# Half of the first batch's x turned by DMA inside the weight fold, with two gate-weight conversions begun later

## The chip, the core and the metric

The kernel runs on one core of a Trainium2 chip. The metric is device time in microseconds: the median of 4 runs of the kernel before is 760.85 us (760.52 to 764.25). The profiler records one execution, which took 760.52 us; its span, from the first to the last recorded instruction, is 758.7 us. Engines are TensorE (PE; its weight loads are shown apart as PEld), VectorE (DVE), ScalarE (ACT), GpSimd (POOL) and SyncE (SP), which here only issues DMAs.

## What is computed

The four weight matrices are 64-bit floats, which the kernel reads as pairs of 32-bit words and converts itself; q, k, v, g_norm and the output are 32-bit. Cut to what matters:

```python
# q, k, v: (8 batches, 8 heads, 576 rows, 64); w1, w2: (512, 1024); w3: (1024, 1024); w_out: (1024, 512)
kv  = einsum('bhsd,bhse->bhde', k, v)
o   = einsum('bhsd,bhde->bhse', q, kv)
o   = o / sqrt(mean(o * o, axis=-1) + 1e-6) * g_norm
x   = o.transpose(0, 2, 1, 3).reshape(4608, 512)
out = ((x @ w1) * (x @ w2)) @ w3 @ w_out
```

## The kernel before, in words

**Stages.** The kernel has a fold, then nine groups of 512 rows of x (eight batches of 512 rows, and one group of the rows left over from all batches). The fold computes w3 @ w_out once, so that each group needs only the two gate products and one projection. The fold has two halves of eight chunks each (`c` from 0 to 7 in `fold_chunk(half, c, ...)`, L615). For each chunk TensorE turns four 128x128 blocks of w3 (`turn_w3`, L602), ScalarE copies them out of PSUM (L607), and TensorE makes four products over 512 columns. In the second half the sums of each quarter are copied to `w3o_sb` (L620) when chunk 7 is done.

**Conversion.** Weights come in 64-bit form through four raw buffers and are converted unit by unit (`conversion`). A unit is begun with two ScalarE passes (L158, L159) by `begin_next` and ended with four VectorE passes (L161, L165, L168, L171) and, for gate weights, a scaling by g_norm (L136 on VectorE, L134 on ScalarE for units begun in the first group) by `end_next`. Counted from 0 there are 20 units: eight chunks of w3 and w_out (0 to 7), then w3's second half and the gate weights in turn; 10, 12, 14, 15, 16, 17, 18 and 19 are gate weights (w1 and w2 for one of eight blocks of columns). In the second half of the fold, units 10 to 15 are begun at the head of chunks 0 to 5.

**The first batch.** The second half of the fold also does the attention of batch 0, since the first group needs its x. At chunks 1 and 4, k times v (L334) and the turning of q (L353) are done for two pairs of heads each; at the ends of chunks 2 and 5 the product with kv (L410), `product(0)` and `product(1)`. Its norm runs on ScalarE and VectorE (L378, L379, L383, L385) and ends with VectorE writing xn (L388), in the next chunk. xn must be turned, so that features lie along partitions. Before the change TensorE does this at the ends of chunks 3 and 6 (`turn`, L444: four 128x128 transposes for each of two r), and ScalarE copies the result to xT (L446). xn has one buffer for both halves.

**Turning by DMA.** Later batches turn x in another way (`x_by_dma`, `turn_by_dma`): a copy that sets the two 16-bit halves of each word apart (L291), a DMA transpose issued by SP (L295), and a copy that puts the halves together again (L305). Two such turns, one for each r, run in step. POOL makes the copies. The first transpose overwrites cells that both first copies read, so it waits for both, and the copies behind wait for both transposes.

**Gates and projection.** A group's two gate products are made together by a scheme with seven block products instead of eight (`winograd`, L636). `combine_x(0)` (L678) and `sum_w(p)` (L688, L689) prepare the sums which it needs. The first products are put in one PSUM bank each and copied out (`keep`, L649, tiles p and u) before another product is added on top in the same bank. Of x, the first product needs only the half h = 0, the second t1 (a difference within h = 0), the third t2, which needs both halves.

**Order.** PE, POOL and SP follow the order of the program text everywhere. Inside the fold VectorE and ScalarE do so too. In the first group (T = 0) VectorE and ScalarE are ordered by a scheduler, which weighs when it expects each instruction's inputs; conversions 16 to 19 are done there. SP is one queue: a DMA that must wait holds all behind it.

Of the kernel before, what the change touches and what calls it, by code (L numbers as in the profile page):

```python
# [22 lines left out]
def kernel(  # L23
# [32 lines left out]
    nc = tc.nc  # L56
    PSUM = bass.MemoryType.PSUM
    P = 128
# [5 lines left out]
    KF = DF // P  # L64
    NH = KF // 2
# [17 lines left out]
    def bank(pool, tag):  # L83
        return pool.tile([P, 512], FP32, name=tag, tag=tag)
# [19 lines left out]
    def load_kv_left(b):  # L104
        for t, src in zip(kv_left, (k, v)):
            nc.sync.dma_start(out=t[0:L], in_=src[b, :, G:S, :].rearrange("h p d -> p h d"))

    def load_q_left(b):
        if b % 2 == 0:
            q_left[b // 2] = inp.tile([P, H, D], FP32, name="ql_sb", bufs=1)  # L110
        nc.sync.dma_start(
            out=q_left[b // 2][(b % 2) * L:(b % 2 + 1) * L],
            in_=q[b, :, G:S, :].rearrange("h p d -> p h d"),
        )
# [105 lines left out]
    def conversions(n):  # L220

        what, i = todo[n]
        if what == "w":
            dst = w_sb[:, i].rearrange("p w c f -> p (w c f)")

            return [conversion(n, dst, raws[n], scale=g_col, by_scalar=in_first_group)]
        if what == "b":
            return [conversion(n, chunks[:, 2 * i:2 * i + 2, 0, :], raws[n])]
        dst = chunks[:, i].rearrange("p w f -> p (w f)")
        cuts = [[0, 256, 512, 1024], [0, 512, 1024], [0, 1024]][min(i, 2)]  # L230
        return [conversion(n, dst, raws[n], slice(a, b)) for a, b in zip(cuts, cuts[1:])]
# [4 lines left out]
    def begin_next():  # L236
        if len(begun) < len(todo):
            begun.append(conversions(len(begun)))
            for c in begun[-1]:
                next(c)  # L240

    def end_next(load=True):
        for c in begun[len(converted)]:
            all_of(c)
        converted.append(len(converted))
        if load:
            load_next()

    def all_of(steps):
        for _ in steps:  # L250
            pass
# [16 lines left out]
    def keep_warm(n):  # L268

        t = bank(ps_mm, "mm")  # L270
        for _ in range(n):
            nc.tensor.matmul(t[:, 0:P], lhsT=ident, rhs=ident, start=True, stop=True)

    def turn_by_dma(srcs, apart, turned, dsts, copy=nc.gpsimd.tensor_copy):

        def words(t):
            return t.bitcast(U16).rearrange("p ... (n w) -> p ... n w", w=2)  # L280

        def planes(t, i, n):
            t = t.bitcast(U16).rearrange("p (w n) -> p w n", w=2)
            size = 4 * P // n
            return t[:, :, i * size:(i + 1) * size]

        for i, src in enumerate(srcs):
            to = planes(apart, i, len(srcs))
            if len(src.shape) == 3:
                src, to = words(src), to.rearrange("p w (a n) -> p w a n", a=src.shape[1])  # L290
                copy(to, src.rearrange("p a n w -> p w a n"))  # L291
            else:
                copy(to, words(src).rearrange("p n w -> p w n"))
        yield
        nc.sync.dma_start_transpose(  # L295
            out=turned.bitcast(U16).rearrange("p (a t) -> p a t", t=P), in_=apart.bitcast(U16)
        )
        yield
        for i, dst in enumerate(dsts):
            src = planes(turned, i, len(dsts))  # L300
            if len(dst.shape) == 3:
                src = src.rearrange("p w (a n) -> p a n w", a=dst.shape[1])
            else:
                src = src.rearrange("p w n -> p n w")
            copy(words(dst), src)  # L305

    def together(turns):

        turns = list(turns)
        while turns:  # L310
            turns = [t for t in turns if next(t, turns) is None]
            yield


    def attention(b):
# [129 lines left out]
            dst = xT[b][:, r // 2, :, r % 2, :]  # L445
            copies["xT"] = nc.scalar.copy(dst, t_ps.rearrange("p (i j) t -> p i (j t)", i=2))  # L446

        def x_by_dma(h):

            xn, x = st[h].rearrange("p i l m d -> p (i l) (m d)"), xT[b][:, h]  # L450
            flat = x.rearrange("p i r n -> p (i r n)")
            turned = st[h].rearrange("p i l m d -> p (i l m d)")
            half = [slice(r * G, (r + 1) * G) for r in range(2)]
            return together(
                turn_by_dma(
                    [xn[:, :, r * P:(r + 1) * P]], flat[:, half[r]], turned[:, half[r]], [x[:, :, r]]
                )
                for r in range(2)
            )
# [138 lines left out]
    def turn_w3(half, c):  # L598
        t_ps = bank(ps_at, "at").rearrange("p (m f) -> p m f", m=NH)
        for m in range(NH):  # L600
            src = chunks[:, c, 0, m * P:(m + 1) * P]
            nc.tensor.transpose(t_ps[:, m, :], src, ident)  # L602

        w3T[half, c] = ab[c % 4 // 2][:, c % 2].rearrange(
            "p i (a f) -> p (i a) f", f=P
        )
        nc.scalar.copy(w3T[half, c], t_ps)  # L607
# [3 lines left out]
    def fold_chunk(half, c, ms):  # L611
        if c == 0 and 0 in ms:
            sums_ps[half] = [bank(ps_mm, "mm") for m in range(NH)]
        for m in ms:
            nc.tensor.matmul(  # L615
                sums_ps[half][m], lhsT=w3T[half, c][:, m, :], rhs=chunks[:, c, 1, :],
                start=(c == 0), stop=(c == KF - 1),
            )
            if c == KF - 1:
                nc.scalar.copy(w3o_sb[:, half * NH + m, :], sums_ps[half][m])  # L620
# [573 lines left out]
    with tc.manual_schedule(  # L1194
        engines={mybir.EngineType.DVE, mybir.EngineType.Activation, mybir.EngineType.SP}
    ):
        for _ in range(RAW):
            load_next()
        nc.scalar.activation(const.tile([P, 1], FP32, name="warm"), eps_col, AF.Sqrt)
        g_row = const.tile([1, P], FP32, name="g_row")  # L1200
        for e in range(2):
            nc.scalar.dma_start(
                out=g_row[:, e * D:(e + 1) * D], in_=g_norm.rearrange("(o d) -> o d", o=1)
            )


        keep_warm(14)
        begin_next()
        end_next()
        turn_w3(0, 0)  # L1210
        keep_warm(5)
        begin_next()

        g_ps = bank(ps_at, "at")[:, 0:1]
        nc.tensor.transpose(g_ps, g_row, ident[0:1, 0:1])
        nc.scalar.copy(g_col, g_ps)
        for c in range(KF):

            if c == 0:
                end_next()  # L1220
                begin_next()
            else:
                begin_next()
                end_next()
            if c == 4:
                load_kv_left(0)
                load_pair("kvq", 0, 0)
            elif c == 5:
                load_pair("kvq", 0, 1)
                load_q_left(0)  # L1230
            fold_chunk(0, c, range(NH - 1))
            turn_w3(*((0, c + 1) if c + 1 < KF else (1, 0)))
            fold_chunk(0, c, [NH - 1])
            if c == 0:
                keep_warm(4)


        first = batch(0)
        first.start()
        BEGIN, PRODUCT = {1: (0, 1), 4: (2, 3)}, {2: 0, 5: 1}  # L1240
        norms = {}
        FIRST = len(converted) + KF - 1
        for c in range(KF):
            if c in BEGIN:
                first.begin_kv(*BEGIN[c])
                first.begin_q(*BEGIN[c])
                if c == max(BEGIN):
                    load_q_left(1)
            if c - 1 in norms:
                all_of(norms[c - 1])  # L1250
            if c < KF - 2:
                begin_next()

                end_next(len(raws) < FIRST)
            elif c == KF - 2:
                run(sum_w(0))
            else:
                run(combine_x(0))
                end_next(False)
                for _ in range(3):  # L1260
                    load_next()
            fold_chunk(1, c, range(NH - 1))
            if c + 1 < KF:
                turn_w3(1, c + 1)
            fold_chunk(1, c, [NH - 1])
            if c in PRODUCT:
                norms[c] = first.product(PRODUCT[c])
                next(norms[c])
                next(norms[c])
            if c - 1 in norms:  # L1270
                for r in range(2):
                    first.turn(2 * PRODUCT[c - 1] + r)
    fold_cm.__exit__(None, None, None)
    late_pool = ctx.enter_context(tc.tile_pool(name="late", bufs=1, reuse_waits="tile"))
    allocate()
# [119 lines left out]
```

## Time and profile before

| what | us |
|---|---|
| median of 4 runs | 760.85 |
| profiled execution, time | 760.52 |
| profiled execution, span | 758.7 |
| TensorE matmuls busy | 751.2 |
| VectorE busy | 586.1 |
| ScalarE busy | 262.1 |
| GpSimd busy | 165.7 |
| first gate matmul (L636) starts at | 83.39 |
| the first group's second, third and fourth gate start at | 95.48, 111.69, 124.74 |

Busy time is the sum of the durations of an engine's instructions. The chain of work that ended last is followed back from the last instruction: at each step to what released it, or to the instruction before it on its engine. A line of the timeline has the start, the time, the engine and line, the operation, the tile written and those read, shapes, a count where equal instructions are merged, and in brackets the idle time ahead of it with what ended it. Each matmul of 32-bit data is seen as two passes in the counts. A window's line has for each engine its busy time and number of instructions, then the granted clock, the DMA engines' mean share and GB/s.

### The profile page before, as it was taken

How to read it: one execution, taken by the hardware profiler on the slowest of the kernel's cores; microseconds unless marked ns; L12 is line 12 of the kernel's file. 1: busy time of each engine (PE TensorE's matmuls, PEld its weight loads, DVE VectorE, ACT ScalarE, POOL GpSimd, SP SyncE). 2: the span in 40 equal slices, each digit the busy share in tenths (PEclk: the TensorE clock that was granted, in tenths of full speed). 3: DMA queues.
4: the chain of work that ended last, by engine and by line, in shares of the span. 5: the costliest groups of instructions: out<-in, count | busy, mean ns of one | idle time of the engine just before them, and what ended most of it. 6: DMA issues, size and time to landing. Idle time of an engine off the chain costs nothing.

```text
span 758.7 us, 14978 instructions
## 1 busy us (share of the span) xinstructions
PE 751.2 (99%) x5923; PEld 658.5 (87%) x5923; DVE 586.1 (77%) x1171; ACT 262.1 (35%) x488; POOL 165.7 (22%) x190
## 2 busy tenths in 40 slices
PE   8999999999999999999999999999999999999998
PEld 5455788888899889988998899889988999999997
DVE  7978999539888568847985898467866778996897
ACT  6677776312322332232223322322233223222321
POOL 0000000222510441043104410431053125006100
PEclk9999999999999999999999999999999999999999
DMA  9996843339997836776677566735742470466244
GB/s 322 337 355 190 224 147 77 84 105 260 309 319 256 230 101 165 230 220 133 204 225 226 142 186 228 220 93 161 231 129 56 150 220 39 146 202 194 84 146 146
DMA packets 142330, 142.15 MB, mean 187 GB/s; under 512 B 82356, under 2 KB 129588, under 8 KB 142260
## 3 DMA queue, kind: packets, MB, share of 16 engines
q1 hardware_dynamic: 139808, 126.77, 56.6%
q10 hardware_dynamic: 2452, 14.42, 5.8%
q8 instruction: 47, 0.77, 0.4%
q14 instruction: 23, 0.19, 0.1%
HBM read 105.78 MB, written 19.14 MB: 165 GB/s over the span
## 4 chain that ended last, share of the span: by engine, by line
PE 96%; DMA 2%; ACT 0%; issue 0%; SPq 0%; DVE 0%; ACTq 0%
PE mm L636 55%; PE mm L1065 22%; PE mm L615 7%; PE mm L865 5%; PE at L334 3%; PE at L410 2%; DMA raw<-in_moe_w_out_dram 1%; DMA w3o_sb<-w3o_l 1%; PE at L865 1%; PE at L602 1%; PE at L1116 0%; DMA raw<-in_moe_w_dram 0%; PE at L444 0%; PE at L353 0%; PE at L429 0%; ACT ab L158 0%
## 5 line engine op out<-in xcount | busy, mean ns | idle before, releaser
L636 PE MATMUL mm<-xT,w_sb 128*128 128x256 f32 x720 | 165.2, 379 | 0.0
L636 PEld LDWEIGHTS mm<-xT,w_sb 128*128 128x128 f32 x720 | 136.3, 190 | 18.7 <-issue 0.5
L636 PE MATMUL mm<-xc,ws 128*128 128x256 f32 x512 | 115.7, 379 | 0.0
L636 PEld LDWEIGHTS mm<-xc,ws 128*128 128x128 f32 x512 | 97.2, 190 | 13.3
L291 POOL COPY xT<-xn 128x1024 uint16<-128x1024 uint16 x26 | 31.4, 1236 | 173.8 <-DVE xn L388 173.8
L774 DVE TENSOR_TENSOR c<-mm,u 128x512 f32<-128x512 f32 x32 | 22.0, 688 | 59.8 <-PE mm L636 59.8
L649 ACT COPY u<-mm 128x512 f32<-128x512 f32 x58 | 34.0, 586 | 95.9 <-PE mm L636 85.4
L649 ACT COPY p<-mm 128x512 f32<-128x512 f32 x66 | 38.8, 588 | 74.4 <-PE mm L636 74.4
L615 PE MATMUL mm<-chunks,ab 128*128 128x512 f32 x128 | 60.3, 603 | 1.3 <-ACT chunks L159 0.8
L636 PE MATMUL mm<-xc,w_sb 128*128 128x256 f32 x256 | 61.5, 383 | 0.0
L636 PE MATMUL mm<-xT,ws 128*128 128x256 f32 x240 | 57.4, 382 | 0.0
L775 DVE TENSOR_TENSOR ab<-c 128x256 f32<-128x256 f32 x96 | 54.0, 562 | 2.5
L636 PEld LDWEIGHTS mm<-xc,w_sb 128*128 128x128 f32 x256 | 47.7, 190 | 7.1 <-ACT u L649 0.3
L636 PEld LDWEIGHTS mm<-xT,ws 128*128 128x128 f32 x240 | 45.0, 190 | 6.3
L379 DVE TENSOR_REDUCE inv<-sq 128x8 f32<-128x512 f32 (+1 forms) x40 | 23.4, 627 | 34.6 <-ACT sq L378 34.6
L1065 PE MATMUL mm<-w3o_sb,ab 128*128 128x128 f32 x368 | 48.7, 275 | 0.2 <-DMA w3o_sb<-w3o_l 0.2
L1065 PE MATMUL mm<-w3o_sb,raw 128*128 128x128 f32 x372 | 48.1, 275 | 0.4 <-DMA w3o_sb<-w3o_l 0.4
L1065 PEld LDWEIGHTS mm<-w3o_sb,ab 128*128 128x128 f32 x368 | 45.4, 192 | 0.8 <-issue 0.4
L1065 PEld LDWEIGHTS mm<-w3o_sb,raw 128*128 128x128 f32 x372 | 44.7, 192 | 0.6 <-issue 0.6
L770 ACT COPY c<-mm 128x256 f32<-128x256 f32 x32 | 12.0, 374 | 93.5 <-PE mm L636 93.5
L305 POOL COPY xT<-xn 128x1024 uint16<-128x1024 uint16 x26 | 32.2, 1267 | 54.3 <-DMA xn<-xT 54.3
L1076 ACT COPY u<-mm 128x512 f32<-128x512 f32 x23 | 13.5, 586 | 86.3 <-DVE raw L1089 38.5
(298 smaller groups left out, 1372.6 us busy)
## 6 DMA issues: line engine op xcount, KB each, us to landing
w3o_sb<-w3o_l SPq DMA_DIRECT2D x18, 896.0 KB, 4.7
raw<-in_moe_w_dram SPq DMA_DIRECT2D x31, 512.0 KB, 7.4
raw<-w3o_l SPq DMA_DIRECT2D x15, 896.0 KB, 4.7
w3o_sb<-w3o_l ACTq DMA_DIRECT2D x14, 896.0 KB, 4.8
k_sb<-in_k_dram SPq DMA_DIRECT2D x32, 256.0 KB, 4.2
v_sb<-in_v_dram SPq DMA_DIRECT2D x32, 256.0 KB, 4.6
q_sb<-in_q_dram SPq DMA_DIRECT2D x32, 256.0 KB, 3.8
out_dram<-raw SPq DMA_DIRECT2D x14, 512.0 KB, 5.0
```

The costliest lines, as they stand in the source:

```text
L291: copy(to, src.rearrange("p a n w -> p w a n"))
L305: copy(words(dst), src)
L334: nc.tensor.matmul(kv_ps[e * D:(e + 1) * D, r - rs[0], :], lhsT=k_sb[:, e, cols] if j < J else kl[:, 2 * r + e, :], rhs=v_sb[:, e, cols] i ...
L379: nc.vector.tensor_reduce(out=inv[:, i], in_=sq.rearrange("p (h d) -> p h d", d=D), axis=AX.X, op=ALU.add)
L410: nc.tensor.matmul(o_ps[l][tokens, n * D:(n + 1) * D], lhsT=qT[r][rows, e, i, tokens], rhs=kv_b[rows, e, r, :], start=True, stop=True,)
L615: nc.tensor.matmul(sums_ps[half][m], lhsT=w3T[half, c][:, m, :], rhs=chunks[:, c, 1, :], start=(c == 0), stop=(c == KF - 1),)
L636: nc.tensor.matmul(ps[:, u, :], lhsT=lhsT(a_name, u, c), rhs=rhs(b_name, c),  start=(u == 0 and c == 0 and to is None), stop=(c == chunks ...
L649: copies.setdefault(name, []).append(nc.scalar.copy(t, ps))
L774: nc.vector.tensor_add(c, one, two)
L775: nc.vector.tensor_mul(dst, c[:, 0, :], c[:, 1, :])
L865: nc.tensor.matmul(ps[place // 4][:, place % 4, :], lhsT=x, rhs=y, start=new and place // 4 not in seen, stop=True, skip_group_check=True,)
L1065: nc.tensor.matmul(to[:, i, :], lhsT=x[:, c, :], rhs=y[:, c, :], start=new and place // 4 not in seen, stop=(c == 1), skip_group_check=True,)
```

## The change

Batch 0's first half of x (h = 0) is turned by DMA with ScalarE in place of POOL for the copies: begun at the end of chunk 3 and ended at chunk 5. The turns of the second half move from the end of chunk 6 into chunk 7, behind its first product; `combine_x(0)`, the end of unit 15 and three loads move behind them. Unit 14 is begun in chunk 4 behind `turn_w3`, not at the head of that chunk; unit 15 is begun in chunk 6, not in chunk 5.

```diff
-        def x_by_dma(h):
+        def x_by_dma(h, copy=nc.gpsimd.tensor_copy):
...
                 turn_by_dma(
-                    [xn[:, :, r * P:(r + 1) * P]], flat[:, half[r]], turned[:, half[r]], [x[:, :, r]]
+                    [xn[:, :, r * P:(r + 1) * P]], flat[:, half[r]], turned[:, half[r]], [x[:, :, r]],
+                    copy,
                 )
...
             if c - 1 in norms:
                 all_of(norms[c - 1])
             if c < KF - 2:
-                begin_next()
+                if c < max(BEGIN):
+                    begin_next()
+                if c == max(BEGIN) + 1:
+                    all_of(x_first)
 
                 end_next(len(raws) < FIRST)
             elif c == KF - 2:
                 run(sum_w(0))
-            else:
+            fold_chunk(1, c, [0])
+            if c + 1 == KF:
+                for r in range(2):
+                    first.turn(2 + r)
                 run(combine_x(0))
                 end_next(False)
                 for _ in range(3):
                     load_next()
-            fold_chunk(1, c, range(NH - 1))
+            fold_chunk(1, c, range(1, NH - 1))
             if c + 1 < KF:
                 turn_w3(1, c + 1)
+            if c in (max(BEGIN), KF - 2):
+                begin_next()
             fold_chunk(1, c, [NH - 1])
             if c in PRODUCT:
                 norms[c] = first.product(PRODUCT[c])
                 next(norms[c])
                 next(norms[c])
-            if c - 1 in norms:
-                for r in range(2):
-                    first.turn(2 * PRODUCT[c - 1] + r)
+            if c - 1 == min(PRODUCT):
+                x_first = first.x_by_dma(0, nc.scalar.copy)
+                next(x_first)
+                next(x_first)
```

`max(BEGIN)` is 4, `min(PRODUCT)` is 2, `KF` is 8 and `NH` is 4.

## The prediction

> **What bounds the kernel now.** I read the page first, parts 1 and 4, for the engine that carries the end:
>
> ```profile
> PE 751.2 (99%) x5923; PEld 658.5 (87%) x5923; DVE 586.1 (77%) x1171; ACT 262.1 (35%) x488; POOL 165.7 (22%) x190
> PE 96%; DMA 2%; ACT 0%; issue 0%; SPq 0%; DVE 0%; ACTq 0%
> ```
>
> TensorE is on 96% of the chain that ended last. So an instruction taken off TensorE is worth its own time, and a copy on another engine costs only what TensorE waits for it. Then the chain in order of time around the change (start, length, what, all in us):
>
> ```profile
> 61.80 0.86 PE mm L615 x2
> 62.66 0.95 PE at L444 x8
> 63.61 1.31 PE at L334 x40
> 64.92 1.02 PE at L353 x8
> 65.94 2.58 PE mm L615 x6
> 68.52 0.44 PE at L602 x4
> 68.96 3.68 PE mm L615 x8
> ...
> 79.10 1.01 PE at L444 x8
> 80.11 3.44 PE mm L615 x8
> 83.55 17.28 PE mm L636 x80
> ```
>
> It is unbroken TensorE from 61.8 to 100.8 us; both groups of L444 (the two pairs of turns of x) lie on it. Eight fold matmul passes take 3.44 us undisturbed and 3.68 where a late ScalarE copy (L607) holds the next chunk. Next, ScalarE's and VectorE's lines in order of time, since the change loads the first and delays the second:
>
> ```profile
> 80.67 1.06 ACT L293 COPY qT<-q_sb 128x1024 uint16<-128x1024 uint16 x1
> 91.98 1.15 ACT L134 ACTIVATE w_sb<-w_sb,g_col 128x1024 f32<-128x1024 f32 x1 [0.15 <-DVE w_sb L171]
> 97.41 0.59 ACT L649 COPY p<-mm 128x512 f32<-128x512 f32 x1 [1.35 <-PE mm L636]
> 104.87 2.23 ACT L305 COPY qT<-q_sb 128x1024 uint16<-128x1024 uint16 x2
> 90.72 1.22 DVE L171 CUSTOM_DVE_ANT_0 w_sb<-w_sb,ab 128x2048 uint16<-128x2048 uint16 x1
> ```
>
> They price the new copies (about 1.05 us apart, 2.23 for two), and show a chain used below: the last pass of a gate unit on VectorE (L171) releases ScalarE's scaling (L134), which stands in ScalarE's queue ahead of the copy p out of PSUM. Last, POOL's timeline in batch 1, where the same turn by DMA stands, and the DMA's share in the window 62 to 64 us:
>
> ```profile
> 148.29 2.23 POOL L305 COPY xT<-xn 128x1024 uint16<-128x1024 uint16 x2 [4.27 <-DMA xn<-xT]
> 62.00:64.00 2.00, 2.00 (x25) 1.35 (x25) 2.00 (x3) 2.00 (x4) 0.00 (x0) 1.00 0.00 0
> ```
>
> A pair of DMA transposes takes 4.27 us from the last copy ahead of it to the first behind it, in a stretch with little traffic (share 0.17 from 140 to 160 us). At 62 to 64 us the DMA engines are idle.
>
> **The Trainium skill.** "ScalarE: Activation LUTs", section "What ACT_TABLE_LOAD costs", gives an ACTIVATE with immediate operands 186 ns + 0.833 ns per element: 1,039 ns for 1,024, as an estimate for a copy. The trace agrees for L293 (1.03 to 1.08 us); L305 on ScalarE is slower (1.16 to 1.19). "TensorE: Matmul & The Clock Gate", section "Part 4: PE-mode transpose", says that a turn on TensorE ends in PSUM and needs a copy out; here that is L446, 0.59 us each. "DMA: Bandwidth & Descriptors", section "Issuing engines are not separate DMA queues", says that all DMAs share 16 engines; so new transposes can be late behind loads, and the trace has transposes landing 2.7 to 10.5 us after issue. "Perfetto Trace Analysis", section "Identifying the Most-Contended Engine", warns that matmul busy time overstates TensorE; the chain and the missing gaps are what I rest on.
>
> **The change part by part** (times of before; the instruction order of the changed program is known, its durations are taken from the rows).
>
> 1. Turns 0 and 1 leave TensorE: 8 transposes, the piece of 0.95 us, which includes a wait for xn (L388). Gain 0.95. The copies L446 (two, 1.07 us) go too.
>
> 2. ScalarE gets two L291-type copies after chunk 4's L607: 63.35 to about 65.35. Never seen on ScalarE; L293's 1.05 is the nearest (POOL does L291 in 1.04 to 1.24), bounds 0.95 to 1.25. Behind them in the queue are the kv copies (65.35 to 66.45) and two qT copies (to 67.4). TensorE needs the kv bank for chunk 5's turn at 68.52 − 0.95 = 67.5, so 1.1 us cover it; without that cover each us late is a us lost.
>
> 3. On SP two transposes go in ahead of batch 1's k and v loads. Both copies must be done (they read what the first transpose overwrites): issue at 65.4 and 66.7, both landed at 65.4 + 4.27 = 69.7. SP is then late for k by about 67.9 − 64.26 = 3.6 us. But before, SP waited between these loads (one v issue took 1.81 us, kl and vl came after a pause), so I put the gate-weight loads behind them at about 72 instead of 71.31; k and v are read at 100.8, the first of those weights at 84.5.
>
> 4. Unit 14's begin (L158, L159) moves behind chunk 5's L607. That copy now runs at 67.9 instead of 69.16, before TensorE needs it: the 3.68 shrinks to about 3.5. Gain 0.16. VectorE is not delayed: it is busy with unit 13 until 70.7 in either kernel, and unit 14's L158 is done by 69.5.
>
> 5. ScalarE then has L305 twice from 70.5 to 72.75, ahead of chunk 6's L607 (to 73.35) and of the squares. TensorE needs that L607 at 73.75. So cover is 0.4 us at the copy, and 0.8 us before the DMA (69.7) would be what ScalarE waits for.
>
> 6. Turns 2 and 3 move into chunk 7 behind its first matmul. VectorE runs unit 14 without a break to 75.25, so xn comes only 0.5 us earlier, at about 78.55; TensorE arrives at 78.65. So they run at about the undisturbed 0.87 (1.01 before): gain 0.14. combine_x(0) follows with t1 at 81.1 and t2 at 81.9, needed at 83.9 and 85.6: nothing. First gate matmul: 83.4 − 0.95 − 0.16 − 0.14 = 82.15, 1.25 us earlier.
>
> 7. The first group. Unit 15's begin is now inside the fold (77.4 to 79.5), and the scheduler puts the rest in another order. Each gate's copy p must leave PSUM before its bank takes the third product. In gate 0 the second copy stands behind unit 16's two passes (84.7 + 1.06 + 1.06, then 0.6: done 87.5), needed at 82.15 + 3 × 1.73 = 87.35: loss 0.2. In gate 1 the first p now stands behind unit 16's L134 and unit 18's L158. On VectorE, unit 16's L171 no longer runs at 90.72: unit 15's four passes start at 83.7, and then L161, L136, L165, four ws sums, two c sums and two products come ahead of it; summing their start-to-start times (1.14 for L161 and L171, 0.6 for most, 0.34 for products) it ends at 95.7. Then L134 1.05, L158 1.06, p 0.6: done 98.45. TensorE would want it at about 97.85. Loss 0.6. From there VectorE, without idle time from 84 to 107 us in the profile, is about 0.7 ahead of its old times, and in gate 2 the copy p (114.42 + 0.57 = 115.0, needed at 113.42 + 1.73 = 115.15) has only 0.15 us of slack before, so more than about 0.8 could not come through anyway.
>
> Sum: −0.95 − 0.16 − 0.14 + 0.2 + 0.6 = −0.45. The profiled execution has a span of 758.7 and a time of 760.52, so 1.8 lies around it and is untouched: 760.1 for it. The median, 760.85, is 0.33 above that execution; I predict 760.4 against the median. After the first group the order on all engines is the old one, so I let the shift pass unchanged to the end; a wait of about 1 us for a load in the second group (TensorE waits for w3o_sb near 228 and 231 us) hangs on loads issued from the same chain and should shift along.
>
> **The rivals.**
> A. The whole 1.25 comes through: the waits of step 7 are small sums of many rows and vanish if VectorE is 0.7 us faster than I sum. For it: before, no such wait shows between 83 and 135 us. Against: L171's new place. 760.85 − 1.25 = 759.6.
> B. VectorE or the later loads hold the old times and all is absorbed, or step 7 is worse by 1 us: 760.85 to 761.6. For it: VectorE has no idle time there, and gate 2's 0.15 us slack. Against: it starts this stretch 0.5 earlier.
> C. Slower: ScalarE's queue is blocked at L305 by the DMA transposes, and L607 with w3T of chunk 6 waits behind it. TensorE loses every us beyond 0.8 + 0.4; the change turns slower once the pair lands over 1.2 + 0.45 = 1.65 us late, that is 5.9 us instead of 4.27 after the copies. With the slowest landing in the trace (10.5 us after an issue at 66.7, so 77.2, against 70.9 that costs nothing) it is +6.3 − 0.45: about 766.7. For it: 0.8 us of slack is thin. Against: the idle DMA window, and the k and v loads are issued after the transposes.
> That the change does not act (the copies remain, or the turns) is excluded: the changed program has 8 transposes less on TensorE.
>
> **How the numbers follow.** Forecast 0.45, A 0.24, B 0.17, C 0.10, and 0.04 for a gain that I cannot name. 0.5% is 3.8 us, about what a measurement of this kernel can tell from no change; forecast, A and B all lie within it, and so does C where the pair lands under some 5 us late, for which I leave it 0.02. Faster by more would need waits of over 3.8 us to vanish: the chain has none such after 15 us. So faster 0.04, within 0.88, slower 0.08. The range takes A with a scatter of 0.6 below it (759.0) and B with the same above (762.2); it leaves out most of C. The runs of before scatter from 760.52 to 764.25, so a median may stand somewhat high.
>
> **What would show it.** Right: no L444 near 62 us, 8 transposes at about 78.7; two L291 copies on ScalarE from 63.4; the two DMA transposes issued at about 65.4 and landed by 70; no TensorE gap near 73.7; L636 beginning near 82.2; a TensorE wait of some tenths before gate 1's third product near 98, with L134 in ScalarE's queue ahead of p. Wrong: L305 starting after 71 with DMA as the releaser (C), a first gate at 83 or later (step 5 or 6), or gate 2 starting 1.2 us earlier than 111.7 (A). If the time moves by over 3.8 us the cause lies outside this stretch, and the reading of the chain as TensorE's own time is wrong.

## The result, and the profile after

The changed kernel takes 760.32 us (median; 759.56 to 761.82) against 761.22 for the kernel before (760.03 to 768.68). The ratio is 0.9984, with a 95% interval of 0.9976 to 0.9992: 1.2 us faster, 0.6 to 1.8, within the 0.5% that I set as the bound of a change that can be told. It is close to the ratio of the means (760.38 and 761.58), in which the longest executions weigh; by medians the kernel is 0.90 us faster. The forecast was 760.4. The two kernels' fastest executions lie 0.5 us apart; what differs most is the upper end, and that is where this study ends up.

The page of the changed kernel, parts 1 and 4:

```profile
PE 751.2 (99%) x5915; PEld 658.3 (87%) x5915; DVE 588.4 (78%) x1171; ACT 264.5 (35%) x490; POOL 164.9 (22%) x190
PE 94%; ACT 2%; DMA 2%; DVE 1%; issue 0%; SPq 0%; ACTq 0%
```

Eight matmul instructions fewer, as said, and yet no less TensorE time. ScalarE and VectorE have come onto the chain. The chain in order of time (start, length, what) shows where:

```profile
62.76 0.86 PE mm L616 x2
63.62 1.32 PE at L334 x40
64.94 1.02 PE at L353 x8
65.96 2.58 PE mm L616 x6
...
68.98 3.52 PE mm L616 x8
...
95.75 1.15 DVE w_sb L171
96.92 0.61 ACT w_sb L134
...
97.98 1.15 ACT ab L158
99.12 0.48 ACT p L650
...
99.65 1.99 PE mm L637 x8
```

L444 is gone from between the fold matmul and L334, and 3.68 has become 3.52. The second part is step 7's chain for gate 1, link by link: VectorE's L171, then ScalarE's L134, L158 and the copy p (L650), then TensorE. ScalarE's timeline of the changed kernel (in brackets idle time and what ended it):

```profile
64.29 2.01 ACT L291 COPY xT<-xn 128x1024 uint16<-128x1024 uint16 x2
...
69.01 0.59 ACT L608 COPY ab<-at 128x512 f32<-128x512 f32 x1 [0.65 <-PE at L603]
...
71.61 2.23 ACT L305 COPY xT<-xn 128x1024 uint16<-128x1024 uint16 x2
73.75 0.59 ACT L608 COPY ab<-at 128x512 f32<-128x512 f32 x1
...
88.10 0.61 ACT L650 COPY p<-mm 128x512 f32<-128x512 f32 x1
...
99.02 1.05 ACT L650 COPY p<-mm 128x512 f32<-128x512 f32 x2
```

L305 starts without a wait for the DMA, so the pair of transposes is hidden; L608 of chunk 6 follows at once. The two copies p at the end are the late ones. TensorE's timeline of the changed kernel, at the product of each gate that waits for such a copy (the fourth of gate 0, the third of gate 1), and then in the second group's projection:

```profile
88.76 1.99 PE L637 MATMUL mm<-xT,ws 128*128 128x256 f32 x8 [0.23 <-ACT p L650]
...
99.65 1.99 PE L637 MATMUL mm<-xc,ws 128*128 128x256 f32 x8 [0.26 <-ACT p L650]
...
228.19 3.29 PE L1066 MATMUL mm<-w3o_sb,raw 128*128 128x128 f32 x28
231.31 1.50 PE L1066 MATMUL mm<-w3o_sb,ab 128*128 128x128 f32 x12
```

TensorE waits in both gates for a copy p, and not at all in the projection. In the profile of before, the timeline has these two lines of the projection instead, with waits for loads of w3o_sb:

```profile
227.89 3.36 PE L1065 MATMUL mm<-w3o_sb,raw 128*128 128x128 f32 x28 [0.41 <-DMA w3o_sb<-w3o_l]
231.46 1.58 PE L1065 MATMUL mm<-w3o_sb,ab 128*128 128x128 f32 x12 [0.21 <-DMA w3o_sb<-w3o_l]
```

The fold's second chunk is the last that has to wait in the opening; its first matmul, called the first fold matmul from here on, starts between 14.62 and 16.04 us in the profiles of this study (15.07 before, 16.04 after). That scatter is larger than the whole effect, so positions are compared from that matmul on. The table is worked out from TensorE's timelines: the first product of each gate and the first matmul of the second group's projection, less that matmul's start; the last columns are TensorE's waits for w3o_sb in the second group, the span less that matmul's start, and the time that SP spends on issuing the two transposes of xn near 195 us.

| kernel | gate 0 | gate 1 | gate 2 | second group | waits for w3o_sb | to the end | SP, pair near 195 |
|---|---|---|---|---|---|---|---|
| before | 68.32 | 80.41 | 96.62 | 202.87 | 0.62 | 743.6 | 4.78 |
| before, again | 68.31 | 80.41 | 96.61 | 202.87 | 0 | 742.6 | 4.08 |
| changed | 67.14 | 79.73 | 96.61 | 202.77 | 0 | 742.9 | 2.78 |
| changed, again | 67.14 | 79.74 | 96.48 | 202.64 | 0 | 742.6 | 2.60 |
| changed, a third | 67.24 | 79.82 | 96.57 | 202.72 | 0.23 | 742.9 | 3.22 |
| turns alone | 69.19 | 81.27 | 97.48 | 203.64 | 0 | 743.8 | 2.93 |
| passes alone | 68.15 | 80.71 | 96.93 | 203.09 | 5.15 | 749.8 | 5.09 |
| before, two small loads | 68.37 | 80.47 | 96.70 | 202.92 | 4.65 | 749.2 | 5.03 |
| changed, six small loads | 67.20 | 81.34 | 97.72 | 203.87 | 0 | 743.6 | 3.21 |
| order 1 | 67.15 | 79.75 | 95.96 | 202.68 | 0 | 742.7 | 3.47 |
| order 2 | 67.42 | 79.59 | 95.79 | 202.42 | 0 | 742.3 | 3.27 |
| order 3 | 67.30 | 79.48 | 95.68 | 202.03 | 0 | 742.1 | 2.64 |
| before, q not turned | 68.29 | 80.38 | 96.58 | 202.83 | 0 | 742.7 | 4.15 |
| changed, q not turned | 67.14 | 79.74 | 96.45 | 202.61 | 0 | 742.4 | 3.00 |

So of the 1.18 us that the fold saves, at most 0.17 is left when gate 2 begins. A gain of 0.9 us in the median must come from somewhere else. That set the two questions: what takes the 1.1 us in the first group, and is the missing wait in the second group an effect of the change?

### The profile page after: what moved, and what is told of

It is laid out like the page before. It is cut to its first block, busy times and chain, and to the rows that moved or that the text cites. A ratio compares the mean times of both kernels' runs of the same rounds, so it can differ in the third digit from the quotient of the medians.

```text
span 758.9 us, 14966 instructions
## 1 busy us (share of the span) xinstructions
PE 751.2 (99%) x5915; PEld 658.3 (87%) x5915; DVE 588.4 (78%) x1171; ACT 264.5 (35%) x490; POOL 164.9 (22%) x190
## 4 chain that ended last, share of the span: by engine, by line
PE 94%; ACT 2%; DMA 2%; DVE 1%; issue 0%; SPq 0%; ACTq 0%
PE mm L637 53%; PE mm L1066 23%; PE mm L616 6%; PE mm L866 5%; PE at L334 3%; PE at L410 2%; DMA raw<-in_moe_w_out_dram 1%; PE at L866 1%; PE at L603 1%; ACT ab L158 1%; PE at L1117 0%; DMA raw<-in_moe_w_dram 0%; ACT w_sb L159 0%; ACT w3o_sb L621 0%; PE at L353 0%
## 5 line engine op out<-in xcount | busy, mean ns | idle before, releaser
L637 PEld LDWEIGHTS mm<-xc,ws 128*128 128x128 f32 x512 | 97.1, 190 | 14.2 <-ACT p L650 1.0
L291 POOL COPY xT<-xn 128x1024 uint16<-128x1024 uint16 x26 | 31.0, 1219 | 174.8 <-DVE xn L388 174.8
L650 ACT COPY u<-mm 128x512 f32<-128x512 f32 x58 | 34.1, 588 | 95.8 <-PE mm L637 84.6
L650 ACT COPY p<-mm 128x512 f32<-128x512 f32 x66 | 38.6, 586 | 73.2 <-PE mm L637 68.1
L305 POOL COPY xT<-xn 128x1024 uint16<-128x1024 uint16 x26 | 31.9, 1255 | 54.2 <-DMA xn<-xT 54.2
```

The source lines that it names most:

```text
L637: nc.tensor.matmul(ps[:, u, :], lhsT=lhsT(a_name, u, c), rhs=rhs(b_name, c),  start=(u == 0 and c == 0 and to is None), stop=(c == chunks ...
L650: copies.setdefault(name, []).append(nc.scalar.copy(t, ps))
```

## The experiments

Theory 1 takes both as effects of the change: its passes cost gates 0 and 1 what the fold gains, and the second group's waits for w3o_sb are gone for good. Its rivals are that those waits are scatter, and that the loss comes from ScalarE's new copies. Theories 2 and 3, on why the waits should have become rarer, came later.

**Both kernels again.** No edit.

> The kernel before, unchanged, profiled a second time: how much of the difference of the two profiles is scatter. Theory 1 (the waits of TensorE for w3o_sb in the second group, 0.41 and 0.21 us near 228 and 231 us, belong to the kernel): they show again, the stretch from the first L1065 of the second group (218.10) to its end at 241.08 is again 22.8 to 23.1 us, and the fold from its first matmul (15.07) to the first gate (83.4) is again 68.3 within 0.1. Rival (they are scatter of the loads): the waits are absent, or differ by more than 0.4 us, and the stretch is as short as 22.0. Time against the runs of before beside it: 0.

> The changed kernel, unchanged, profiled a second time. Theory 1 (the 1.2 us of the fold are lost again in gates 0 to 2, and the time falls because the load waits of the second group are gone): first matmul to first gate 67.1, first gate to gate 2's first product 29.5 (before 28.3), second group's projection again 22.0 us with no wait for w3o_sb, time -1.2 us within 0.7. Rival (the missing load wait is scatter): the projection takes 22.8 to 23.1 us here and the time is that of before within 0.5 us.

Before: 761.19 us, ratio to before 1.0001 (0.9985 to 1.0017), and its profile shows no wait for w3o_sb. Changed: 760.19 us, ratio 0.9986 (0.9976 to 0.9995), no wait either. So the gain repeats, and so does the loss in gates 0 and 1, but the 0.62 us of waits in the one profile of before aren't always there: the rival is right on them. In these two profiles, neither of which has such a wait, the kernels take the same time from the first fold matmul to the end, 742.6 us each (742.9 in the first profile of the changed kernel, also without one). What the first comparison of two profiles showed as a clean exchange was partly chance, and the mechanism has to be sought in how often and how long TensorE waits there.

**The turns alone.** The passes are begun where the kernel before begins them:

```diff
             if c < KF - 2:
-                if c < max(BEGIN):
-                    begin_next()
+                begin_next()
...
-            if c in (max(BEGIN), KF - 2):
-                begin_next()
```

> The changed kernel with the passes of the gate units begun where the kernel before begins them: only the turn of x by DMA with ScalarE's copies and the turns of the other half in the last chunk are left of the change. Theory 1 (the passes' new place costs what gates 0 and 1 lose): first gate 0.9 to 1.1 us earlier against the first fold matmul; no wait for p of over 0.1 us before the third product of gates 0 and 1, so that gate 1 starts about 0.9 earlier; gate 2 then loses what exceeds its slack of 0.15 us unless VectorE is also earlier. Time 0.3 to 1.0 us under the changed kernel if VectorE is earlier too, equal to it if gate 2 takes the gain back. Rival (the loss in gates 0 and 1 comes from ScalarE's four new copies or the DMA, whatever the passes' place): the same waits of 0.2 to 0.4 us before the third products as in the changed kernel.

761.2 us, ratio to before 0.9999 (0.9985 to 1.0014). TensorE's timeline:

```profile
71.04 2.84 PE L616 MATMUL mm<-chunks,ab 128*128 128x512 f32 x6 [1.15 <-ACT ab L608]
...
76.79 2.84 PE L616 MATMUL mm<-chunks,ab 128*128 128x512 f32 x6 [0.52 <-ACT ab L608]
```

And ScalarE's:

```profile
68.29 1.18 ACT L158 ACTIVATE ab<-raw 128x1024 f32<-128x1024 uint32 x1
69.35 1.16 ACT L159 ACTIVATE w_sb<-raw 128x1024 f32<-128x1024 f32 x1
70.40 0.59 ACT L608 COPY ab<-at 128x512 f32<-128x512 f32 x1
...
72.91 1.22 ACT L159 ACTIVATE w_sb<-raw 128x1024 f32<-128x1024 f32 x1
73.97 2.27 ACT L305 COPY xT<-xn 128x1024 uint16<-128x1024 uint16 x2
76.11 0.63 ACT L608 COPY ab<-at 128x512 f32<-128x512 f32 x1
```

I expected the first gate about 1 us earlier than before; it comes 0.87 later. The two L291 copies push the passes, and the passes and then L305 stand ahead of the copy L608 that the next chunk needs. ScalarE, busy 35% of the span, is the bound of the fold here. Behind it, gates 0 and 1 run without waits for p and are as long as before (12.08 and 16.21 us). Theory 1 takes that as proof that their loss comes from the passes' place, but for gate 1 ScalarE's timeline says otherwise:

```profile
97.86 1.15 ACT L134 ACTIVATE w_sb<-w_sb,g_col 128x1024 f32<-128x1024 f32 x1
98.92 1.15 ACT L158 ACTIVATE ab<-raw 128x1024 f32<-128x1024 uint32 x1
99.97 0.56 ACT L650 COPY p<-mm 128x512 f32<-128x512 f32 x1
```

Unit 16's scaling and unit 18's L158 stand ahead of the first copy p here too. The copy is done at 100.53 us; TensorE, 1.5 us later in gate 1 than in the changed kernel, wants it at 98.97 + 1.73 = 100.70 and just finds it. So the wait is missing because TensorE is late, and this run doesn't tell the passes' place from the turns. Although gate 2 begins 0.86 us later than before, the median is that of before. That would fit a time given back behind gate 2, as in the changed kernel, but the interval, about 1.1 us to either side, doesn't show it.

**The passes alone**, on the kernel before with all turns on TensorE:

```diff
             if c < KF - 2:
-                begin_next()
+                if c < max(BEGIN):
+                    begin_next()
...
+            if c in (max(BEGIN), KF - 2):
+                begin_next()
```

> The kernel before with only the place of the passes of two gate units changed as in the changed kernel; all turns of x stay on TensorE. Theory 1: chunk 5's fold matmuls shrink from 3.68 to about 3.5 us and the first gate comes 0.1 to 0.2 earlier; L134 of unit 16 stands behind the last VectorE pass at about 95.7 us and the copy p of gate 1 behind it, but TensorE comes 1.0 us later than in the changed kernel, so that it finds p ready or waits 0.1 at most; gate 2 within 0.1 us of before; time -0.2 to +0.2 us of before. Rival (the order of VectorE's passes costs TensorE time by itself): gate 2 starts 0.4 to 1.1 us later than before and the time is 0.4 to 1.1 us up.

761.65 us, ratio 0.9996 (0.9972 to 1.0019): the time tells nothing. The profile does. The first gate is 0.17 earlier (step 4's 0.16), gate 1 has no wait, but gate 0 has one of 0.21 us, and gate 2 begins 0.31 later than before. Neither expectation holds: gate 0 alone costs more than the fold gains. It is 0.47 us longer than before, nearly as in the changed kernel (0.50), so its loss does come with the passes' place. Gate 1's loss shows in neither of the two halves of the change; it needs TensorE to come as early as both together bring it. The execution profiled also shows how bad the waits in the second group can be:

```profile
228.59 3.36 PE L1065 MATMUL mm<-w3o_sb,raw 128*128 128x128 f32 x28 [0.34 <-DMA w3o_sb<-w3o_l]
236.77 2.90 PE L1065 MATMUL mm<-w3o_sb,ab 128*128 128x128 f32 x12 [4.81 <-DMA w3o_sb<-w3o_l]
```

5.15 us of waits, and a span of 765.4. The long wait is for a load that SP issued at 228.45 us instead of near 225, because the two transposes of batch 3's q had held it from 222.22 to 228.35. Executions like this one would make the upper end of the times of before; none of that kernel's own long executions was profiled.

**Is it the completion semaphores?** SP's DMAs take eight semaphores in turn, and the changed kernel's two additional DMAs shift every later one by two. To shift them and nothing else, small loads that nobody reads went onto SP's queue: two in the kernel before, six in the changed one.

```diff
+    pads = [const.tile([P, 4], FP32, name=f"pad{i}") for i in range(2)]
+
+    def shift_lanes():
+        for t in pads:
+            nc.sync.dma_start(out=t, in_=k[0, 0, 0:P, 0:4])
...
+            if c == 3:
+                shift_lanes()
```

> The kernel before with two small loads (128x4 elements that nobody reads) put on SP's queue where the changed kernel has its two transposes; nothing else is moved on any engine. Every later DMA of SP then gets the completion semaphore (one of eight, taken in turn) that it has in the changed kernel. Theory 2 (the gain of the changed kernel comes from this shift: with it the second load of q near 194 us lands 4 us after its issue instead of 5.5 to 6.5, SP goes on 1.4 to 1.8 us after the issue of the second transpose of xn instead of 2.9 to 3.9, and the loads of w3o_sb in the second group are in time): time 0.5 to 1.2 us under before, no run far above the median, no wait for w3o_sb. Theory 1 (the gain needs the edits of the fold): time within 0.4 us of before, SP goes on after 2.9 to 3.9 us as in the two profiles of before.

> The changed kernel with six more such small loads on SP behind its two transposes, so that with these eight DMAs every later DMA has the completion semaphore that it has in the kernel before; nothing else is moved. Theory 2: SP waits again 2.9 to 3.9 us after the second transpose of xn near 197 us, the second group's loads come late in some runs, and the time is that of before within 0.5 us, with some runs far above the median. Theory 1: 0.8 to 1.3 us under before, as the changed kernel, and SP goes on after 1.4 to 1.8 us.

The first takes 761.8 us, ratio 1.002 (1.0001 to 1.0038), up to 769.82, with 4.65 us of waits in its profile, and SP needs 5.03 us for the pair near 195 us. Long executions are more frequent in it and not rarer: 9 of 22 take over 762.6 us, against 5 of 67 of the kernel before beside it. The second takes 760.56, ratio 0.9999 (0.9979 to 1.0019), up to 766.93, with 3.21 us for the pair. Theory 2 falls on both sides: the pair's time and the waits don't follow the semaphores. The second kernel also shows the cover of step 3: the six loads put off the gate weights, which come 3.2 us later against the first fold matmul (first issue at 77.50 instead of 74.97). ScalarE then waits 1.26 us for a weight at 87.0 us, the copy p stands behind, and TensorE loses 1.79 us in gate 0. Since ScalarE would have begun those passes 0.4 us later than in the changed kernel even without that wait, the cover there is about 3.2 − 1.26 − 0.4 = 1.5 us.

**Is it the transposes of q?** In the second group SP issues two transposes of batch 3's q at about 220 us, and ScalarE issues an 896 KB load at about 222. The view of 3 us windows (of its columns: TensorE's busy time first, and at the end the granted clock, the DMA engines' share and GB/s), for the kernel before with two small loads, and behind it TensorE's timeline at the wait:

```profile
216.00:219.00 3.00, 3.00 (x17) 2.64 (x16) 2.71 (x7) 0.00 (x0) 0.00 (x0) 1.00 1.01 418
...
222.00:225.00 3.00, 3.00 (x30) 3.00 (x28) 2.97 (x5) 1.06 (x2) 2.20 (x2) 1.00 1.23 167
225.00:228.00 3.00, 3.00 (x29) 3.00 (x28) 2.72 (x7) 1.06 (x2) 0.24 (x1) 1.00 1.10 245
228.00:231.00 3.00, 0.40 (x4) 0.21 (x2) 2.69 (x8) 0.48 (x1) 0.00 (x0) 1.00 1.45 104
...
234.00:237.00 3.00, 3.00 (x17) 3.00 (x17) 0.43 (x1) 0.00 (x0) 0.00 (x0) 0.53 1.02 421
```

```profile
233.05 4.99 PE L1071 MATMUL mm<-w3o_sb,raw 128*128 128x128 f32 x28 [4.65 <-DMA w3o_sb<-w3o_l]
```

From 222 to 231 us the DMA engines' share is above 1 (the packets' times overlap in it), and they move only 104 to 245 GB/s; in the last of these windows TensorE stands. From 216 to 219 us, with bulk traffic nearly alone, they move 418. The wait also costs more than its length: behind it the granted clock is 0.53 from 234 to 237 us, and the 28 matmul instructions take 4.99 us instead of 3.29 in the changed kernel. By the table, 749.2 − 742.6 − 4.65 = 1.9 us come on top of it. The second transpose of q, issued at 222.00, landed at 233.31, the load issued at 222.40 at 232.91. The Trainium skill, "DMA: Bandwidth & Descriptors", section "Latency and other measured facts", gives a DMA transpose 261 GB/s where its middle dimension is not contiguous, and about 350 to 400 otherwise; this stretch, in which a load runs too, lies below both. So these two transposes were left out and the copies around them kept (the one behind reads the same cells in another order; batch 3's result is no longer that of the formula):

```diff
-        nc.sync.dma_start_transpose(
+        if send: nc.sync.dma_start_transpose(
...
-            return turn_by_dma([q_sb], to, q_sb, [to], q_copy)
+            return turn_by_dma([q_sb], to, q_sb, [to], q_copy, (b, r) not in ((3, 0), (3, 1)))
```

> The kernel before without the two DMA transposes of batch 3's q that SP issues near 219.5 and 220.9 us (the copies on POOL around them stay, so that part of the computation, the turn of this half of q, is left out; no other instruction moves on any engine). Theory 3 (TensorE's waits for w3o_sb in the second group come from these two transposes meeting the 896 KB load that ScalarE issues near 222 us, and the gain of the changed kernel is mostly that it meets them less often): no wait for w3o_sb, no run over 762.5 us, and a median 0.5 to 1.2 us under before, near the fast end of its runs. Rival (the waits come from the loads' own amount or from earlier in the stream): waits for w3o_sb and runs over 762.5 us remain, time within 0.3 us of before.

> The changed kernel with the same two transposes of batch 3's q left out. Theory 3: the time is that of the changed kernel within 0.4 us and only 0.1 to 0.4 us under the kernel before with the same left out, since the edits of the fold alone are worth 0.10 to 0.23 us by the second group. Rival (the fold's 1.2 us reach the end): 0.8 to 1.3 us under the kernel before with the same left out.

> The changed kernel once more, as the measure for the other three on this chip: 0.5 to 1.3 us under before, no run over 762.5 us.

Against 761.22 us for before (up to 767.83) the kernel before without them takes 760.44 (up to 762.58), ratio 0.9986 (0.9974 to 0.9998). The changed kernel takes 760.22 both with them (ratio 0.9982, 0.9973 to 0.9990) and without them (0.9983, 0.9972 to 0.9994). The windows of before without them:

```profile
222.00:225.00 3.00, 3.00 (x29) 3.00 (x28) 2.93 (x5) 0.94 (x3) 2.01 (x2) 1.00 0.61 220
225.00:228.00 3.00, 3.00 (x29) 3.00 (x29) 2.70 (x8) 0.96 (x2) 0.00 (x0) 1.00 0.90 287
228.00:231.00 3.00, 3.00 (x29) 3.00 (x29) 2.75 (x6) 0.48 (x1) 0.00 (x0) 1.00 0.85 299
```

TensorE never stands here. One profile without a wait proves little, since the second one of before has none either; the times weigh more. They bear theory 3 out: before gains 0.78 us and loses its upper end (the 762.58 misses the expected 762.5 by little; above 762.6 are 12 of 74 runs of before and none of 22 here), the changed kernel gains nothing, and of the difference between the two medians 0.22 us is left. That agrees with the table at the second group (0.10 to 0.23), though medians of 22 runs scatter by more than that. Leaving out two DMAs also shifts the later semaphores, but the runs with small loads speak against that as the reason. So the larger part of the measured gain is that the changed kernel's load there meets these transposes less often, or less badly.

Why it does is open. In the table, the pair of transposes near 195 us takes SP 4.08 to 5.09 us in all five profiles of kernels that turn x's first half on TensorE, and 2.60 to 3.47 in all nine of kernels that turn it by DMA, whatever the passes, the semaphores or the shift in time. But the changed kernel with six small loads has the short pair and still executions up to 766.93, so that pair isn't the whole reason, and what two transposes at 66 us change at 195 us no view shows.

**What ScalarE's order costs.** Three versions of the changed kernel, each adding one reordering. The diff is cut from order 3, which has all three. Order 1 issues unit 16's scaling and unit 18's L158 behind gate 1's first copy p; order 2 also issues unit 16's passes behind gate 0's second copy p; order 3 also issues the square root of batch 1's norm in gate 2 behind its first copy p.

```diff
+                if p == 1:
+                    with tc.issue_after(copies["p1"][1].ins):
+                        late_scale.pop()()
...
-                        ahead = [copies["xT"] if p == 0 else copies["u3"][0], copies["u2"][p]][n]
+                        ahead = [copies["p5"][0] if p == 0 else copies["p1"][1], copies["u2"][p]][n]
...
-        fs[1] += [(a.begin_kv, 2, 3), (a.finish, 0)]
+            fs[1].append((lambda: (rest.append(a.product(0)), next(rest[0])),))
...
+            def rest_of_norm():
+                with tc.issue_after(copies["p1"][-1].ins):
+                    next(rest[0])
+                all_of(rest[0])
```

> The changed kernel, with ScalarE's scaling of unit 16 (L134) and the begin of unit 18 (its L158) issued behind the first copy p of gate 1 instead of ahead of it. Theory (step 7: the 0.42 us that gate 1 loses are that copy's place in ScalarE's queue): no wait of over 0.1 us before gate 1's third product, gates 1 to 2 as long as before (16.2 us), and gate 2 0.3 to 0.4 us earlier against the first fold matmul; if it holds to the end, 0.3 to 0.5 us under the changed kernel. Rival (VectorE, without idle time there, is the limit): the wait goes but gate 2 begins where it did within 0.1 us, because a copy or a product of gate 2 is late by as much.

> As the kernel with the first copy p of gate 1 put ahead, and also the two passes L158 of unit 16 behind the second copy p of gate 0. Theory (both waits of step 7 are ScalarE's order): no wait for p in gates 0 and 1, gate 1 begins 1.1 to 1.2 us earlier than in the kernel before against the first fold matmul (0.7 in the changed kernel), and gate 2 0.6 to 1.1 us earlier; the time 0.5 to 1.0 us under the changed kernel. Rival (VectorE is the limit behind them): gate 2 begins at most 0.3 us earlier and the time is that of the changed kernel within 0.3 us.

> As the kernel with ScalarE's two reorderings for gates 0 and 1, and in gate 2 also the square root of batch 1's norm (L386, which waits for VectorE until 113.4 us) put behind the first copy p instead of ahead of it. Theory (each gate loses only what ScalarE's order costs it): the wait of 0.20 us before gate 2's third product goes, the second group's first product comes 0.2 us or more earlier than with two reorderings (202.4 us after the first fold matmul), time 0.9 to 1.3 us under the changed kernel. Rival (VectorE, busy throughout, takes it back later in gate 2 or 3): the second group's start stays at 202.4 within 0.1 and the time at 0.6 to 0.9 us under the changed kernel.

Order 1 takes 760.34 us where before takes 760.64, ratio 0.9988 (0.9978 to 0.9999); order 2 takes 759.52 beside it, 0.9983 (0.9973 to 0.9994). The changed kernel was not timed beside these two. Order 2 is 0.82 us under order 1, though its second group begins only 0.26 us earlier in the table; where the rest comes from is open. In both, gate 1's wait goes, in order 2 gate 0's too, though gate 1 begins only 0.82 us earlier than before and not the expected 1.1 to 1.2, since the first gate itself is 0.28 later than in the changed kernel, inside the fold. Gate 2 begins 0.5 to 0.65 us earlier than in the changed kernel in order 1, 0.7 to 0.8 in order 2. But then gate 2 has the wait, in order 1:

```profile
115.47 1.99 PE L640 MATMUL mm<-xc,ws 128*128 128x256 f32 x8 [0.30 <-ACT p L653]
```

and 0.20 us of it in order 2. That is the small slack of gate 2 that step 7 named. The place in ScalarE's timeline of order 2:

```profile
113.39 0.31 ACT L386 ACTIVATE inv<-inv,eps_col 128x16 f32<-128x16 f32 x1 [1.48 <-DVE inv L382]
113.61 1.05 ACT L653 COPY p<-mm 128x512 f32<-128x512 f32 x2
```

ScalarE sits 1.48 us at a square root that waits for VectorE, with a copy ready behind it. Order 3 turns these two round:

```profile
112.95 0.59 ACT L665 COPY p<-mm 128x512 f32<-128x512 f32 x1 [0.48 <-PE mm L652]
113.98 0.31 ACT L386 ACTIVATE inv<-inv,eps_col 128x16 f32<-128x16 f32 x1 [0.45 <-DVE inv L382]
```

The wait goes, and the second group begins at 202.03 instead of 202.42. Order 3 takes 759.68 us, ratio to before 0.9978 (0.9966 to 0.9991), 0.54 us under the changed kernel's 760.22 beside it. That is less than either expectation for the time (0.9 to 1.3, or 0.6 to 0.9), and near the 0.6 to 0.7 by which its second group begins earlier. It has the lowest median of the kernels timed beside the 761.22 of before.

## Why the prediction was right, and where not

**Steps 1 to 6 hold**, with positions less 0.97 us for the later start. L334 follows the fold matmul 0.96 us earlier (step 1: 0.95). Two L291 copies on ScalarE take 2.01 us (step 2: about 2.0). The transposes are issued at 66.32 − 0.97 = 65.35 (step 3: 65.4) and L305 finds them landed. 3.68 becomes 3.52 (step 4: 3.5). L305 ends and L608 follows at 72.78 (step 5: 72.75). Turns 2 and 3 take 0.88 us in chunk 7 (step 6: 0.87). The first gate is 1.18 us earlier (1.25). In step 3 the gate weights were put at 72 and are issued at 74.0: that was 2 us off and cost nothing, with some 1.5 us of cover left.

**Step 4 is right as a sum and too small as a reading.** It valued the later begin of unit 14 at 0.16 us. With the turns on ScalarE, the later begins of units 14 and 15 are worth 69.19 − 67.14 = 2.05 us together, because they clear ScalarE's queue for the copies that the turns bring. The step priced the two edits apart and their sum without asking what each is worth once the other is made.

**Step 7 names the right waits and has gate 0's size wrong.** Gate 0 grew from 12.09 to 12.59 us: 0.50 lost, not 0.2. Unit 16's passes began at 85.96 − 0.97 = 85.0, not 84.7, and a product that follows an idle time is followed by the next 1.83 us later, not 1.73 (below), which I left out. Gate 1 grew from 16.21 to between 16.74 and 16.88: 0.53 to 0.67 lost, as forecast (0.6). In sum 1.0 to 1.2 instead of 0.8, so that the fold's gain is nearly gone at gate 2, where I had 0.45 left. VectorE, which I put about 0.7 us ahead of its old times behind gate 1's passes, is 0.3 ahead (L161 at 98.07 − 0.97 = 97.1 instead of 97.4). That the rest could hardly pass gate 2 was right with ScalarE's order as it is: order 1 shows it, and order 3 gets more through by changing that order.

**The step that failed is the sentence after the sum**: that the load wait in the second group "should shift along". It doesn't hang on the position of the compute alone: it varies from one execution to the next, from 0 to over 5 us, and removing the two transposes of q removes it and 0.78 us of the median of before. I took one profile's 0.6 us there (about 1 in my text) for a fixed part of the kernel.

So the forecast of 760.4 is near 760.32 by luck, in two ways. The gain is twice the 0.45 that I forecast, 0.90 by medians: 0.1 to 0.2 us of it from the fold, and most of the rest from a wait that I held fixed. And I took the gain off 760.85, the median of 4 runs of before, where 64 runs have 761.22; these 0.37 us nearly make up for the gain that I missed. The gain, 0.90 by medians and 1.2 by the ratio, is nearer to rival A's 1.25 than to my 0.45, but not by A's mechanism: the waits of step 7 are there. B is right that nearly all of the fold's gain is absorbed in the first group, but not that VectorE holds the old times: with ScalarE's order changed, gate 2 begins 0.94 us earlier than before in order 3. It is wrong on the time. C didn't occur: L305 never waited for the DMA, in any of the nine profiles that have x's first half turned with ScalarE.

## What to carry to other kernels

When work moves to a lightly loaded engine, ask of every copy in its queue who waits for it: ScalarE at 35% was the bound in the fold and in three gates, each time by the order of its queue, and once by a square root that waited for VectorE ahead of a copy that was ready. Price two edits together as well as apart where they share a queue. And before a wait for a load is taken as fixed, profile the same kernel again: a microsecond that comes and goes can be the larger part of a measured gain, and a long wait can cost more than its length.

## What was not expected of the hardware

- In the bad case, with DMA transposes beside bulk loads, the DMA engines were slow while they showed as busy: 104 to 167 GB/s in 3 us windows at a share of 1.23 to 1.45, against 418 for bulk traffic at 1.01. A transpose of q took 2.8 to 3 us to land when it was issued well ahead of the load (221.04 for an issue at 218.24 in order 3), 5.6 to 6.1 us in five profiles where the load followed within 1 us, and 11.3 us in the bad case, with the load beside it at 10.5 us instead of 5.0. The order of issue was the same in those five and in the bad case, so it doesn't explain the difference.
- Behind waits of 4.65 and 4.81 us TensorE's granted clock fell to about half for some 3.5 us (0.50 from 234 to 236 us with two small loads, and from 237 to 239 with the passes alone), and each execution lost about 2 us more than it waited (1.9 and 2.05 by the table). Behind the 0.21 us near 231 us in the profile of before it stayed at 1.00.
- A product that had to wait for its PSUM bank took 1.99 us and the next one started 1.83 us after it, where others take 1.89 and 1.73. So each such wait cost 0.10 us on top of the idle time shown. It doesn't take a wait for the bank: in the profile of before, the products at 102.07 and 109.86 us, which follow matmuls of another kind (L334, L410) and wait for nothing that the timeline shows, have the same 1.99 and 1.83.
- The first fold matmul behind the opening moved between 14.62 and 16.04 us from profile to profile, with the opening unchanged.
